# Z and the output stage of a convolution and token-mixing kernel moved from whole-array matmuls to four 64x64 tiles

## The chip, the core and the metric

The kernel runs on one core of one Trainium2 chip. The metric is the device time of that core in microseconds (us), lower is better. It is given as the median of several executions. Fast executions of one kernel agree here within about 1% (the kernel before on one chip: 180.46 to 182.05 us in seven); some fall into a slower state, with a lower granted TensorE clock in the records (the share of its full clock that the profile says it was given; 0.742 in a run of before of 209.52 us, 0.940 to 0.967 in fast runs of 180.46 to 182.05), or simply a longer time.

## The reference, cut to what matters

```python
batch, seq, d_model, kernel_size, n_heads, d_hyper = 8, 4224, 192, 7, 8, 64

def conv(x, weight):                    # causal convolution, 7 taps, one filter per head of 24 columns
    w = softmax(weight, axis=-1)
    x_pad = concat([zeros(B, 6, D), x], axis=1)
    ...
    return einsum('hk,bskhg->bshg', w, x_unf).reshape(B, S, D)

def mlp(x, w_q, w_k, w_out):            # x is the result of conv
    wq, wk = x @ w_q, x @ w_k
    W_tok = 1 / sqrt(64) * einsum('bsd,btd->bst', wq, wk)
    mixed = einsum('bst,btd->bsd', W_tok, x)
    return relu(mixed) @ w_out          # float32
```

There is no softmax over tokens, so the kernel never forms the 4224 x 4224 matrix. With G = x^T x (192 x 192), `mixed` is (x w_q)(w_k^T G) scaled. Per batch the stages are:

- **Y**: the convolution, as a matmul with a banded matrix.
- **G**: the Gram matrix of Y, summed in one bank of PSUM, the memory that this kernel's matmuls write to (`ps` in the profile). (SBUF is the on-chip memory that they read from: `y`, `zt`, `wall` and others.)
- **T**: Y transposed on VectorE (`STREAM_TRANSPOSE` in the profile, 1,348 ns for 128 x 1,152), to be read in blocks of 32 rows.
- **Q**: w_q^T Y^T, on array tiles of 32 x 64.
- **M**: the 64 x 192 product of w_k and G.
- **Z**: relu(M^T Q), 192 rows for each token.
- **O**: Z^T w_out, the output.

Of the kernel before, what the change touches and what calls it, by code (L numbers as in the profile page):

```python
# [14 lines left out]
KEYS = {  # L15
    "Y": (-0.34, 0.15), "T": (-0.03, 1.15), "Q": (0.07, 0.82), "G": (-0.01, 0.83),
    "Z": (1.01, 0.97), "O": (1.22, 0.93),
}
# [95 lines left out]
def bass_lightweight_conv__then__hypermixer_token_mlp_kernel(  # L114
# [24 lines left out]
    NX = 6  # L139
    NO = 8  # L140
# [19 lines left out]
    ZT = sbuf("zt", [128, NZ, 3, 512], BF16)  # L160
    OUT = sbuf("o_sb", [128, NO, 2, 4 * D], F32)
    GS = sbuf("gs", [128, 512], BF16)
    G12T = sbuf("g12t", [128, 128], BF16)
    M_SB = sbuf("m_sb", [128, 2, 2 * D], BF16)
    BAND = sbuf("band", [128, H, 128], BF16)
    IDENT = sbuf("ident", [128, 128], BF16)
    WST = sbuf("wst", [128, 4, D], F32)
    WALL = sbuf("wall", [128, 1088], BF16)
# [13 lines left out]
    WO1, WO2 = WALL[:, 512:704], WALL[:, 704:1088]  # L182
# [7 lines left out]
    og = [P.group(f"o{i}") for i in range(NO)]  # L190

# [40 lines left out]
    for s, (src, wd) in enumerate(((wk_t, DH), (wo_t, D))):  # L232
        wload(2 * s, 0, 128, src, 0, wd, wl[s + 1])
        wload(2 * s + 1, 0, 64, src, 128, wd, wl[s + 1])
        wload(2 * s + 1, 64, 128, src, 128, wd, wl[s + 1])
# [122 lines left out]
    for o, i, g in (  # L358
        (WO1, WST[:, 2, :], wl[2]),
        (WO2[0:64, 0:D], WST[0:64, 3, :], wl[2]),  # L360
        (WO2[64:128, D : 2 * D], WST[64:128, 3, :], wl[2]),
        (dup(WK1), twice(WST[:, 0, 0:DH]), wl[1]),
        (dup(WK2), twice(WST[:, 1, 0:DH]), wl[1]),
        (dup(WK2A)[0:64], twice(WST[0:64, 1, 0:DH]), wl[1]),
        (dup(WK2B)[64:128], twice(WST[64:128, 1, 0:DH]), wl[1]),
    ):
        wos.append(cast("pool", o, i, g, [wos[-1]]))
    wos.append(pool(lambda e: e.memset(M_SB[:, :, :], 0.0), [wos[-1]]))

# [3 lines left out]
        dve(lambda e: e.memset(ZT[:, :, :, 64:128], 0.0)),  # L373
# [10 lines left out]
    class Job:  # L384
        def __init__(self, name, key, banks, pe, pe_us, reads=(), after=(), evacs=(), then=None,
                     groups=()):
            self.name, self.key, self.banks, self.pe, self.pe_us = name, key, banks, pe, pe_us
            self.reads, self.after, self.evacs, self.then = reads, after, evacs, then
            self.groups = groups
# [64 lines left out]
    def job_q(b, g):  # L454
# [20 lines left out]
        for i0, i1 in ((0, 2), (2, 3), (3, 4)):  # L475
# [30 lines left out]
            after=[("ZD", b - 2, i, h) for i in range(5) for h in range(2)]  # L506
            + [("ZS", b - 2, i) for i in range(5)],
            evacs=evacs,
# [35 lines left out]
    def job_mm(b):  # L544
        def pe(e, bk):
# [11 lines left out]
            after=[("ZD", b - 2, i, h) for i in range(5) for h in range(2)]  # L557
            + [("ZS", b - 2, i) for i in range(5)],
            evacs=[(lambda bk: [
                (M_SB[0:64, b % 2, 0:192], PS[0:64, bk, 0:192]),  # L560
                (M_SB[64:128, b % 2, 256:384], PS[64:128, bk, 0:128]),
                (M_SB[64:128, b % 2, 192:256], PS[64:128, bk, 128:192]),
            ], ("M", b), 480, False, "scale")],
        )

    def blocks(b):
        return (0, 1, 2, 3, 4) if b < B - 1 else (3, 4, 0, 1, 2)

    def nth(b, i):
        return 5 * b + blocks(b).index(i)  # L570

    def zspan(i):
        return (512 * i, 512 if i < 4 else HALF - 2048)

    def zreads(b, i):
        s0, w = zspan(i)
        k = (0, 0, 2, 3, 3)[i]
        q = [("Q", b, 1, 0), ("Q", b, 1, 2)] if i > 2 else []
        return [("M", b), ("Q", b, 0, k), ("Q", b, 1, k)] + q

    def zring_after(n):
        bb, k = divmod(n - NZ, 5)
        ii = blocks(bb)[k]
        return [("O", bb, ii, q) for q in range(2 if ii < 4 else 1)]

    def job_zd(b, i, h):
        s0, w = zspan(i)
        n = nth(b, i)

        def pe(e, bk):  # L590
            return e.matmul(PS[:, bk, 0:w], M_SB[:, b % 2, 256 * h : 256 * h + 128],  # L591
                            QT[:, b % 2, s0 : s0 + w], start=True, stop=True)

        return Job(
            ("ZD", b, i, h), b + KEYS["Z"][0] + KEYS["Z"][1] * (3 * (n % 5) + h) / 15, 1, pe,
            0.42e-3 * w, reads=zreads(b, i), after=zring_after(n),
            evacs=[(lambda bk: [(ZT[:, n % NZ, h, 0:w], PS[:, bk, 0:w])],
                    ("ZD", b, i, h), w, False, "relu")],
        )

    def job_zs(b, i):
        s0, w = zspan(i)
        n = nth(b, i)

        def pe(e, bk):
            return e.matmul(PS[:, bk, 0:w], M_SB[:, b % 2, 128:256], QT[:, b % 2, s0 : s0 + w],  # L606
                            start=True, stop=True)

        return Job(
            ("ZS", b, i), b + KEYS["Z"][0] + KEYS["Z"][1] * (3 * (n % 5) + 2) / 15, 1, pe, 0.42e-3 * w,  # L610
            reads=zreads(b, i), after=zring_after(n),
            evacs=[(lambda bk: [(ZT[:, n % NZ, 2, 0:w], PS[:, bk, 0:w])],
                    ("ZS", b, i), w, False, "relu")],
        )

    def job_o(b, i, q):
        n = nth(b, i)
        zr, orr = n % NZ, n % NO
        rem = i == 4

        def pe(e, bk):
            kw = dict(skip_group_check=True)
            for j in range(1 if rem else 2):
                r = 2 * q + j
                cols = slice(0, 128) if rem else slice(r, 512, 4)
                o = PS[:, bk + j, :]
                for h in range(2):
                    e.matmul(o[:, 192 * h : 192 * h + 192], ZT[:, zr, h, cols], WO1,  # L628
                             start=h == 0, stop=False, **kw)
                last = e.matmul(o[:, 0:384], ZT[:, zr, 2, cols], WO2, start=False, stop=True, **kw)  # L630
            return last

        def make(bk):
            if rem:
                return [(OUT[0:64, orr, :, 0:192],
                         PS[0:64, bk, 0:384].rearrange("p (h d) -> p h d", h=2))]
            return [(
                OUT[:, orr, :, 384 * q : 384 * q + 384].rearrange("p h (r d) -> p r h d", r=2),
                PS[:, bk : bk + 2, 0:384].rearrange("p r (h d) -> p r h d", h=2),
            )]  # L640

        def then():
            halves = n == 5 * B - 1
            if not rem and q == 0 and not halves:
                return
            evs = [o for k in range(q if halves else 0, q + 1) for o in made[("OUT", b, i, k)]]
            row = lambda h, t: (b * S + h * HALF + t) * D
            chunk = [[4 * D, 8], [1, 4 * D]]
            for h in range(2):
                if rem:  # L650
                    parts = [(0, 64, row(h, 17 * CW), [[D, 64], [1, D]])]
                elif halves:
                    parts = [(0, 128, row(h, 32 * i + 2 * q),
                              [[CW * D, 16], [4 * D, 8], [1, 2 * D]])]
                elif i < 3:
                    parts = [(0, 128, row(h, 32 * i), [[CW * D, 16]] + chunk)]
                else:
                    parts = [
                        (0, 96, row(h, 96), [[CW * D, 16], [4 * D, 6], [1, 4 * D]]),
                        (96, 126, row(h, 16 * CW), [[4 * D, 30], [1, 4 * D]]),  # L660
                        (126, 128, row(h, 17 * CW + 64), [[4 * D, 2], [1, 4 * D]]),
                    ]
                for p0, p1, at, dims in parts:
                    src = OUT[p0:p1, orr, h, 0 : D if rem else 4 * D]
                    if halves:
                        src = OUT[:, orr, h, 2 * q * D : 2 * q * D + 2 * D]
                    st = P.dma(
                        "sp",
                        lambda e, src=src, at=at, dims=dims: e.dma_start(
                            bass.AP(out_t, at, dims), src  # L670
                        ),
                        og[orr], evs,
                    )
            st.end = max(o.end for o in evs) + 5.0
# [3 lines left out]
            ("O", b, i, q), b + KEYS["O"][0] + KEYS["O"][1] * (2 * (n % 5) + q) / 9, 1 if rem else 2,  # L678
            pe, 0.33 if rem else 0.655,
            reads=["wo", ("ZD", b, i, 0), ("ZD", b, i, 1), ("ZS", b, i)],  # L680
            evacs=[(make, ("OUT", b, i, q), 384 if rem else 768, False, "copy")],
# [5 lines left out]
        "O": [job_o(b, i, q) for b in range(B) for i in blocks(b)  # L687
              for q in range(2 if i < 4 else 1)],
        "Z": [j for b in range(B) for i in blocks(b)
# [207 lines left out]
```

## The kernel before: the parts that the change touches

A sequence is cut into two halves of 2,112 tokens. Q of one half lies on partitions 0 to 63, that of the other on 64 to 127. Z has 192 rows, which is one and a half times the 128 partitions. The kernel before makes it with three matmuls for 512 tokens of both halves: rows 0 to 127 of the first half, rows 0 to 127 of the second, and rows 128 to 191 of both together. M is padded with zeros, so that one half's M meets zeros in the other half's Q.

```python
def job_zd(b, i, h):          # 128 rows of Z for one half; job_zs: the last 64 rows of both
    def pe(e, bk):
        return e.matmul(PS[:, bk, 0:w], M_SB[:, b % 2, 256 * h : 256 * h + 128],
                        QT[:, b % 2, s0 : s0 + w], start=True, stop=True)
    ...
        evacs=[(lambda bk: [(ZT[:, n % NZ, h, 0:w], PS[:, bk, 0:w])], ..., "relu")]

def job_o(b, i, q):
    def pe(e, bk):
        for j in range(1 if rem else 2):
            r = 2 * q + j
            cols = slice(0, 128) if rem else slice(r, 512, 4)       # every 4th token: step of 8 bytes
            o = PS[:, bk + j, :]
            for h in range(2):
                e.matmul(o[:, 192 * h : 192 * h + 192], ZT[:, zr, h, cols], WO1, ...)
            last = e.matmul(o[:, 0:384], ZT[:, zr, 2, cols], WO2, ...)   # WO2: zeros beside the weights
        return last
```

In this output matmul Z is the stationary operand (the "weights" that are loaded into the array, `LDWEIGHTS ps<-wall,zt` in the profile) and w_out is streamed. Each partition of the output buffer collects four successive tokens, so one store row is 4 x 192 x 4 = 3,072 bytes, and a store takes all 128 partitions:

```python
parts = [(0, 128, row(h, 32 * i), [[CW * D, 16], [4 * D, 8], [1, 4 * D]])]
```

The order of all instructions is fixed when the kernel is built: a list planner in the kernel takes, again and again, the job that is ready and has the lowest key. `KEYS` gives each stage its lead or lag in batches:

```python
KEYS = {"Y": (-0.34, 0.15), "T": (-0.03, 1.15), "Q": (0.07, 0.82), "G": (-0.01, 0.83),
        "Z": (1.01, 0.97), "O": (1.22, 0.93)}
...
rank = (0, job.key) if t <= free["pe"] + 0.05 else (1, t)
```

The kernel takes PSUM as eight banks (`ps`, [128, 8, 512] in float32): G holds bank 7, Q takes four in a row, Y and O take pairs, a Z step takes one.

## Time and profile before

| | before |
|---|---|
| median of 3 runs | 182.16 us (182.05 to 182.72) |
| profiled run | 209.52 us, granted clock 0.742: a slow run |
| a later profile of the same kernel | 181.0 us, granted clock 0.966 |

The first profile is a slow run, and the prediction had only that one. I therefore profiled the kernel before again (run `c_before` below). The profile after was taken in a fast run, so "before" in comparisons of profiles means `c_before`.

How to read the lines: PE is TensorE's matmuls, PEld its weight loads, DVE VectorE, ACT ScalarE. Numbers are us unless they are means of one instruction (ns). The page of the slow profile of before, span, busy time by engine and the chain of waits by engine:

```profile
span 207.8 us, 4686 instructions
...
PE 186.9 (90%) x1911; PEld 125.5 (60%) x1934; DVE 144.9 (70%) x217; ACT 140.4 (68%) x286; POOL 46.6 (22%) x74
...
PE 76%; DMA 8%; DVE 4%; POOL 3%; issue 2%; ACT 2%; SPq 1%; POOLq 0%
```

The table of windows of the same profile, one batch in the middle (its columns are named in its first line):

```profile
core 0: us, PE busy (x) PEld busy (x) DVE busy (x) ACT busy (x) POOL busy (x), PEclk, DMA share, GB/s
105.11:127.53 22.42, 22.06 (x244) 15.29 (x255) 17.13 (x24) 16.91 (x37) 0.00 (x0) 0.75 0.74 180
```

At a clock of 0.75 TensorE alone sets the batch: 22.06 of 22.42 us. The same kernel undisturbed, page of `c_before`; in the lines of the queues the columns are packets, MB and the time that the packets took as a share of 16 engines' span:

```profile
span 179.2 us, 4709 instructions
...
PE 155.2 (87%) x1934; PEld 106.2 (59%) x1934; DVE 143.1 (80%) x217; ACT 136.0 (76%) x286; POOL 46.5 (26%) x74
...
q1 hardware_dynamic: 12016, 26.30, 44.4%
q8 instruction: 15, 0.25, 0.5%
...
PE 46%; DVE 19%; DMA 9%; issue 8%; ACT 6%; POOL 3%; SPq 1%; POOLq 0%
```

Its table of windows, one batch and the end after the last evacuation:

```profile
core 0: us, PE busy (x) PEld busy (x) DVE busy (x) ACT busy (x) POOL busy (x), PEclk, DMA share, GB/s
98.70:116.80 18.10, 17.99 (x240) 12.89 (x239) 16.84 (x24) 16.27 (x37) 0.00 (x0) 1.00 1.33 280
169.00:179.00 10.00, 0.00 (x0) 0.00 (x0) 0.00 (x0) 0.00 (x0) 0.00 (x0) 0.57 0.78 251
```

Here a batch takes 18.1 us, with TensorE busy 99%, VectorE 93% and ScalarE 90% of it. All three are nearly full. The last 10 us only store. Three groups of instructions of `c_before` that the change replaces (count, then busy time and mean ns of one): the output's weight loads, and the ReLU on each engine:

```profile
L796 ACT ACTIVATE zt<-ps 128x512 bf16<-128x512 f32 x59 | 35.0, 639 | 0.3 <-PE ps L606 0.3
...
L628 PEld LDWEIGHTS ps<-wall,zt 128*128 128x128 bf16 x272 | 27.3, 114 | 15.1 <-DVE y L793 2.0 <-issue 1.9 <-ACT o_sb L793 1.5
...
L798 DVE TENSOR_SCALAR zt<-ps 128x512 bf16<-128x512 f32 x37 | 24.6, 682 | 4.6 <-PE ps L591 4.2
```

### The profile page before, as it was taken

The numbers are of one execution on the slowest core, as the hardware profiler recorded it, in microseconds if no ns is written. First come the engines' busy times: TensorE is split into PE (matmuls) and PEld (weight loads), VectorE is DVE, ScalarE is ACT, GpSimd is POOL, SyncE is SP. The second block draws the span as 40 slices with busy tenths as digits, with TensorE's granted clock in tenths as the row PEclk, the third lists the DMA queues.
The fourth block names the chain that finished last, engine by engine and source line by source line (L and its number), as shares of the span: only waits on it lengthen the run. The fifth ranks groups of instructions, "written<-read, shape, count | busy, mean of one in ns | idle before, by whom it ended". The sixth has DMA issues, their size and how long they took to land.

```text
span 207.8 us, 4686 instructions
## 1 busy us (share of the span) xinstructions
PE 186.9 (90%) x1911; PEld 125.5 (60%) x1934; DVE 144.9 (70%) x217; ACT 140.4 (68%) x286; POOL 46.6 (22%) x74
## 2 busy tenths in 40 slices
PE   7769679999998999999999999999999999999920
PEld 2227435776684667666776676766867677676610
DVE  4894838958894489657975799468965797567410
ACT  2555458668967598667975797669876797567720
POOL 7509999997331000000000000000000000000000
PEclk9776767777777777777777777777777777777775
DMA  5990999999999999999999653383247345459676
GB/s 59 190 149 12 158 189 192 191 192 265 289 276 240 269 265 265 263 230 312 258 237 247 189 153 114 84 278 100 89 143 212 103 143 171 137 171 281 189 251 228
DMA packets 49030, 40.44 MB, mean 195 GB/s; under 512 B 39280, under 2 KB 41072, under 8 KB 49008
## 3 DMA queue, kind: packets, MB, share of 16 engines
q0 software_dynamic: 36992, 13.83, 56.2%
q1 hardware_dynamic: 12016, 26.30, 39.8%
q8 instruction: 15, 0.25, 0.5%
q14 instruction: 7, 0.06, 0.1%
HBM read 28.00 MB, written 25.95 MB: 260 GB/s over the span
## 4 chain that ended last, share of the span: by engine, by line
PE 76%; DMA 8%; DVE 4%; POOL 3%; issue 2%; ACT 2%; SPq 1%; POOLq 0%
PE ps L401 13%; PE ps L628 13%; PE ps L630 12%; PE ps L464 8%; PE ps L515 8%; PE ps L516 6%; DMA xw<-in_x_dram 6%; PE ps L591 6%; PE ps L517 4%; PE ps L606 4%; DVE qt L793 3%; DMA wst<-in_moe_w_out_dram 2%; SPq L220 1%; POOL wall L326 1%; POOL xw L205 1%
## 5 line engine op out<-in xcount | busy, mean ns | idle before, releaser
L791 DVE STREAM_TRANSPOSE yb<-y 128x1152 bf16<-128x1152 bf16 x48 | 62.3, 1348 | 0.4
L793 ACT COPY o_sb<-ps 128x768 f32<-128x768 f32 (+1 forms) x59 | 45.3, 768 | 18.5 <-PE ps L630 16.7
L628 PE MATMUL ps<-wall,zt 128*128 128x192 bf16 x272 | 52.7, 282 | 1.7 <-ACT o_sb L793 0.9
L630 PE MATMUL ps<-wall,zt 128*128 128x384 bf16 x136 | 52.6, 387 | 0.0
L793 ACT CAST y<-ps 128x864 bf16<-128x864 f32 (+3 forms) x76 | 39.7, 586 | 11.4 <-PE ps L401 10.2
L515 PE MATMUL ps<-y 128*128 128x192 bf16 x144 | 40.1, 284 | 2.7 <-DVE y L793 1.3
L401 PE MATMUL ps<-xw,band 126*128 126x432 bf16 x128 | 37.9, 424 | 3.7 <-DMA xw<-in_x_dram 2.4
L628 PEld LDWEIGHTS ps<-wall,zt 128*128 128x128 bf16 x272 | 30.4, 121 | 16.2 <-issue 4.6
L516 PE MATMUL ps<-y 128*128 128x192 bf16 x144 | 40.0, 285 | 0.0
L796 ACT ACTIVATE zt<-ps 128x512 bf16<-128x512 f32 (+1 forms) x76 | 36.7, 535 | 2.4 <-PE ps L606 1.2
L798 DVE TENSOR_SCALAR zt<-ps 128x512 bf16<-128x512 f32 (+1 forms) x44 | 26.1, 613 | 14.0 <-PE ps L591 9.5
L517 PE MATMUL ps<-y 128*128 128x128 bf16 x144 | 35.8, 248 | 0.0
L205 POOL DMA_DIRECT2D xw<-in_x_dram x32 | 30.2, 1005 | 8.5 <-issue 7.7
L793 ACT CAST qt<-ps 128x64 bf16<-128x64 f32 (+4 forms) x46 | 15.0, 397 | 17.1 <-PE ps L464 17.1
L793 DVE CAST y<-ps 128x864 bf16<-128x864 f32 x20 | 21.0, 1052 | 6.5 <-PE ps L401 5.1
L591 PE MATMUL ps<-qt,m_sb 128*128 128x512 bf16 (+1 forms) x59 | 21.0, 393 | 1.2 <-issue 0.8
L401 PEld LDWEIGHTS ps<-xw,band 126*128 126x128 bf16 x128 | 12.3, 107 | 15.5 <-issue 4.0
L516 PEld LDWEIGHTS ps<-y 128*128 128x128 bf16 x144 | 16.1, 112 | 8.9 <-issue 7.3
L793 DVE COPY o_sb<-ps 128x768 f32<-128x768 f32 (+1 forms) x13 | 11.6, 895 | 13.3 <-PE ps L630 13.3
L515 PEld LDWEIGHTS ps<-y 128*128 128x128 bf16 x144 | 15.9, 110 | 8.3 <-issue 2.8
L464 PE MATMUL ps<-yb,wq 32*64 32x288 bf16 x768 | 18.1, 328 | 0.0
L793 DVE CAST qt<-ps 128x224 bf16<-128x224 f32 (+6 forms) x42 | 7.9, 253 | 12.9 <-PE ps L464 12.9
(64 smaller groups left out, 148.3 us busy)
## 6 DMA issues: line engine op xcount, KB each, us to landing
out_dram<-o_sb SPq DMA_DIRECT2D x46, 384.0 KB, 4.2
xw<-in_x_dram POOLq DMA_DIRECT2D x24, 384.0 KB, 20.1
out_dram<-o_sb SPq DMA_DIRECT2D x16, 288.0 KB
xw<-in_x_dram POOLq DMA_DIRECT2D x8, 432.0 KB, 20.2
out_dram<-o_sb SPq DMA_DIRECT2D x16, 90.0 KB
out_dram<-o_sb SPq DMA_DIRECT2D x16, 48.0 KB, 4.9
out_dram<-o_sb SPq DMA_DIRECT2D x4, 192.0 KB
xw<-in_x_dram POOLq DMA_DIRECT2D x16, 29.2 KB, 23.5
```

Source lines behind the costliest of these rows:

```text
L205: return e.dma_start(XW[0:rows, b % NX, slot : slot + n, :], bass.AP(x_t, base, [[D, rows], [CW * D, n], [1, D]]),)
L401: last = e.matmul(PS[:, k + j, 0:432], BAND[0 : 6 + CW, h, :], rhs, start=True, stop=True)
L464: last = e.matmul(PS[64 * h : 64 * h + 64, bk + i, 0:288], WQ[r, j, :], rhs, start=j == 0, stop=j == 5, skip_group_check=True)
L515: e.matmul(PS[:, 7, 0:192], y[:, 0:128], y[:, 0:192], start=c == 0, **fl)
L516: e.matmul(PS[:, 7, 192:384], y[:, 256:384], y[:, 192:384], start=False, **fl)
L517: return e.matmul(PS[:, 7, 384:512], y[:, 128:256], y[:, 128:256], start=False, **fl)
L591: return e.matmul(PS[:, bk, 0:w], M_SB[:, b % 2, 256 * h : 256 * h + 128], QT[:, b % 2, s0 : s0 + w], start=True, stop=True)
L628: e.matmul(o[:, 192 * h : 192 * h + 192], ZT[:, zr, h, cols], WO1, start=h == 0, stop=False, **kw)
L630: last = e.matmul(o[:, 0:384], ZT[:, zr, 2, cols], WO2, start=False, stop=True, **kw)
L791: last = e.transpose(o, i)
L793: last = e.copy(o, i) if eng == "act" else e.tensor_copy(o, i)
L796: last = e.activation(o, i, AF.Relu)
```

## The change

Both Z and O multiply by zeros: Z contracts over 64 rows but uses 128, O contracts over 192 rows but spends the array on 256. The change cuts the array into four 64x64 tiles that hold no zeros. Z is made in three parts of 64 rows (`j`); in each, the array's two row halves take the two sequence halves (`h`) and its two column halves take two blocks of 512 tokens (`g`), so one step is four matmuls at once. The output is summed over the three parts, again with four tiles at once. Each output partition now collects eight successive tokens, so a store row is 6,144 bytes, and a store takes 64 partitions. M needs no padding, and the ReLU empties two banks (1,024 columns) with one instruction. To pay for larger units in memory, the input ring `NX` shrinks from 6 to 5 batches; the output ring keeps its bytes with half as many units of double size. The order keys were set anew, with a penalty for a change of array mode, which is the way the array is cut into tiles.

```diff
 KEYS = {
-    "Y": (-0.34, 0.15), "T": (-0.03, 1.15), "Q": (0.07, 0.82), "G": (-0.01, 0.83),
-    "Z": (1.01, 0.97), "O": (1.22, 0.93),
+    "Y": (-0.82, 0.03), "T": (0.08, 0.78), "Q": (0.17, 0.82), "G": (-0.04, 0.43),
+    "Z": (0.92, 0.82), "O": (1.35, 0.93), "mode": (0.11, 0.13),
 }
-    NX = 6
-    NO = 8
+    NX = 5
+    NO = 4
-    ZT = sbuf("zt", [128, NZ, 3, 512], BF16)
-    OUT = sbuf("o_sb", [128, NO, 2, 4 * D], F32)
+    ZT = sbuf("zt", [128, NZ, 3, 2, 512], BF16)
+    OUT = sbuf("o_sb", [128, NO, 2, 8 * D], F32)
 ... (head: one load of w_out into 64 rows, fewer casts, no padding of M; all else about weights cut)
+    def job_z(b, u, j):
+        def pe(e, bk):
+            for h in range(2):
+                r = slice(64 * h, 64 * h + 64)
+                for g in range(2):
+                    c = 512 * (2 * u + g)
+                    last = e.matmul(PS[64 * g : 64 * g + 64, bk + h, :],
+                                    M_SB[r, b % 2, 64 * j : 64 * j + 64],
+                                    QT[r, b % 2, c : c + 512], start=True, stop=True, ...)
+            return last
+ ...    evacs=[(lambda bk: [(ZT[:, n % NZ, j, :, :], PS[:, bk : bk + 2, :])],
+                ("Z", b, u, j), 1024, False, "relu")],
 ... (job_zr, job_or: the last 64 tokens of each half, the same way)
+    def job_o(b, u, k):
+        v, q = divmod(k, 2)
+        def pe(e, bk):
+            for rr in range(2):
+                for j in range(3):
+                    for h in range(2):
+                        for g in range(2):
+                            p = slice(64 * g, 64 * g + 64)
+                            last = e.matmul(
+                                PS[64 * h : 64 * h + 64, bk + g, 192 * rr : 192 * rr + 192],
+                                ZT[p, zr, j, h, slice(4 * v + 2 * q + rr, 512, 8)],
+                                WO[p, j, :], start=rr == 0 and j == 0, stop=j == 2, ...)
 ... (then(): stores after the fourth output step, 64 partitions each)
+                        c = [[CW * D, 16], [8 * D, 4 if i < 3 else 3], [1, 8 * D]]
+                        parts.append((OUT[64 * h : 64 * h + m, orr, g, :], row(h, 32 * i), c))
-            rank = (0, job.key) if t <= free["pe"] + 0.05 else (1, t)
+            change = 0.0
+            if job.pe and job.mode != mode[0]:
+                change = KEYS["mode"][0]
+                t += 0.1
+            rank = (0, job.key + change) if t <= free["pe"] + 0.15 else (1, t)
```

## The prediction

> **What bounds the kernel now.** The profiled run is a slow one (span 207.8 us, granted clock 0.742; the timed runs took 182.16). In it TensorE bounds everything between the head and the tail: in the table of windows each batch repeats every 22.42 us with TensorE busy 22.0, VectorE 17.1, ScalarE 16.9; the chain of waits is 76% TensorE. I count 39,744 streamed columns per batch (band filter 6,912, Gram 9,216, Q 3,456, Z 6,336, output 13,056, rest 768). In the timeline an output pair of 768 columns repeats every 0.43 us, 1.79 columns per ns; so 39,744 columns are 22.2 us, and almost nothing is left for mode changes or gaps. The head (first matmuls of batch 1 at 27 us, waiting for x, which was issued after the weights' casts) and the store tail (199.5 to 207.8) hardly follow the clock. So a fast run has (180.4-36)/7.67 = about 18.8 us per batch. There VectorE and ScalarE (34.0 us together, 17.0 each) are 90% busy and TensorE is about as full: three engines bind together.
>
> **What the change removes.** Z needs 6 x 512 columns plus a remainder instead of 6,336, output 17 x 576 instead of 17 x 768: 6,300 columns per batch, 16%: 3.5 us at the slow clock, about 2.6 at the full one. This needs four 64x64 tiles to run together; [...]the Q stage agrees here: 48 matmuls of 288 columns on 32x64 tiles took 1.14 us, so eight overlapped.
>
> Evacuation: the elements stay, instructions fall. Six pairs of 512-wide ReLU (ScalarE 617 ns, VectorE 688) become 1,024 wide (extrapolated from 512 and 768 wide: 0.99 and 1.23 us), saving 0.15 to 0.25 us each; three remainders become one, three M copies one: together about 1.9 us of 34 per batch, 0.95 per engine.
>
> Head: two weight loads, a 0.74 us memset and some casts leave the chain before x of batch 1: -1 us.
>
> **What it adds.** Three array modes[...]. Four changes per batch cost at most 0.34 us now (22.42-22.08), 0.085 each; I expect 10 to 16: about 1 us. Weight loads: 24 small ones per output step instead of 6, reading Z every 16 bytes instead of 8; loads now take 113 ns strided against 98 contiguous, so a coarser stride may cost more. Z takes bank pairs, so while Q holds four banks only one pair is left. Tail: the last stores leave in 0.75 MB pieces rather than 0.38 MB, at 360 GB/s: +1 us.
>
> **On the critical path.** TensorE per batch (fast) about 14 + 1 = 15; evacuation 16 per engine. Evacuation becomes the bound; at 92% use a batch takes 17.3 us instead of 18.8: 7.67 x 1.5 = -11.5; head -1, tail +1. Predicted 170.5 us, range 162 to 179; faster by over 2% 0.80, within 2% 0.12, slower 0.08.
>
> **What would show it.** Right: batch period (slow clock) 19 to 20 us; four output matmuls starting within one 192-column time; VectorE and ScalarE over 85% busy; ReLU of 1,024 near 1.0 and 1.2 us; TensorE idle waiting for evacuation. Wrong: an output step well above 0.64 us at the slow clock (weight loads bound it), gaps over 0.1 us at mode changes, long waits for free banks.
>
> **What would make it wrong.** Weight loads not hidden or serial between tiles (then output gains nothing and it may be slower); mode changes of 0.2 us or more; the after profile in another clock state; a tail longer than 10 us.

Beside it:

- -11.5 - 1 + 1 from 182 gives 170.5.
- That tiles overlap rested on the Q stage: in the first profile the 48 matmuls of a Q step start in groups of eight within 24 ns, and the groups follow one another after 123 to 173 ns.
- The price of 0.085 us for a change of mode and the +1 us for the tail are estimates: 0.34 us of a batch over four changes, and 0.37 MB more at the rate of the tail of before (windows of the first profile: 371 GB/s from 200 to 202 us, 359 from 202 to 204).
- That head and tail hardly follow the clock held for the head: the first band matmuls of batch 1 start at 27.0 us in the slow profile and in `c_before`. From the last matmul to the end it is 9.5 and 11.7 us.

## The result, and the profile after

| | before | after |
|---|---|---|
| median | 182.21 us, 4 runs | 213.85 us, 4 runs |
| ratio of fast runs | | 1.170 (1.161 to 1.178) |
| span of the fast profile | 179.2 (`c_before`) | 212.6 |
| granted clock in it | 0.966 | 0.932 |

The change made the kernel 17% slower. A ratio is the mean time of one kernel's fast runs over that of the other's in the same rounds, so it is not quite the ratio of the medians that I quote. One of the four runs after (218.04 us) is slow and is left out of it. Experiments ran on chips 2, 3 and 5 (the record doesn't name the chip of this pair), each beside runs of the kernel before; differences to after are therefore given by the medians and, in brackets, by the ratios, as a share of 182 us.

The page of after, the lines that answer to those of `c_before`:

```profile
span 212.6 us, 7380 instructions
...
PE 166.0 (78%) x3326; PEld 115.7 (54%) x3326; DVE 132.9 (63%) x192; ACT 140.9 (66%) x231; POOL 46.1 (22%) x72
...
q1 hardware_dynamic: 7840, 26.25, 46.0%
q8 instruction: 26, 0.43, 0.8%
...
PE 63%; DMA 9%; ACT 6%; DVE 5%; POOL 4%; issue 4%; SPq 1%; POOLq 0%
```

No engine is full any more: VectorE is busy 63%, ScalarE 66%. The instruction queue carries 26 packets instead of 15, beside 3,326 matmuls and as many loads on TensorE instead of 1,934. The windows of after, four batches and the end:

```profile
core 0: us, PE busy (x) PEld busy (x) DVE busy (x) ACT busy (x) POOL busy (x), PEclk, DMA share, GB/s
71.40:94.80 23.40, 20.42 (x415) 14.25 (x413) 15.60 (x22) 17.45 (x29) 0.00 (x0) 0.93 1.38 260
94.80:119.90 25.10, 20.70 (x415) 14.54 (x413) 15.47 (x22) 17.32 (x29) 0.00 (x0) 0.93 0.83 182
119.90:140.60 20.70, 19.22 (x415) 13.72 (x413) 15.44 (x22) 17.06 (x29) 0.00 (x0) 1.00 0.66 159
140.60:161.20 20.60, 19.37 (x415) 13.82 (x413) 15.51 (x22) 17.16 (x29) 0.00 (x0) 1.00 0.66 158
195.00:212.00 17.00, 0.00 (x0) 0.00 (x0) 0.00 (x0) 0.00 (x0) 0.00 (x0) 0.57 0.79 197
```

Two kinds of batch stand out: calm ones of 20.6 us at the full clock, and two of 23.4 and 25.1 us, at a clock of 0.93, in which x is still arriving (its last packet starts at 106.3 us, halfway through the second). The tail, in which only stores run, is 17 us instead of 10, at 197 GB/s instead of 251. The groups of instructions of after:

```profile
L632 PE MATMUL ps<-wo,zt 64*64 64x192 bf16 x1536 | 57.7, 287 | 2.3 <-DVE zt L839 0.8 <-DVE qt L834 0.8 <-issue 0.3
...
L632 PEld LDWEIGHTS ps<-wo,zt 64*64 64x64 bf16 x1536 | 51.3, 209 | 10.4 <-issue 1.9 <-ACT o_sb L834 1.3 <-DVE zt L839 1.3
...
L837 ACT ACTIVATE zt<-ps 128x1024 bf16<-128x1024 f32 x43 | 44.0, 1029 | 12.8 <-PE ps L587 12.1
...
L587 PEld LDWEIGHTS ps<-qt,m_sb 64*64 64x64 bf16 x192 | 6.1, 113 | 15.2 <-ACT o_sb L834 6.1 <-issue 3.7 <-ACT zt L837 2.2
...
L839 DVE TENSOR_SCALAR zt<-ps 128x1024 bf16<-128x1024 f32 x5 | 6.1, 1224 | 3.8 <-PE ps L587 3.8
```

Compare the two kinds of 64x64 load: one of Z's weights (contiguous, line 587) takes 113 ns, one of the output's (every eighth token, line 632) takes 209. The timeline of TensorE in after, a calm stretch and a disturbed one (start, duration, then what ran; consecutive equal instructions are joined):

```profile
start us, us, engine line op out<-in xcount [idle before <-releaser]
...
127.14 0.22 PE L524 MATMUL ps<-y 128*128 128x128 bf16 x1
127.30 1.68 PE L632 MATMUL ps<-wo,zt 64*64 64x192 bf16 x48
128.80 0.39 PE L587 MATMUL ps<-qt,m_sb 64*64 64x512 bf16 x4
...
97.33 0.40 PE L587 MATMUL ps<-qt,m_sb 64*64 64x512 bf16 x1
100.91 0.41 PE L587 MATMUL ps<-qt,m_sb 64*64 64x512 bf16 x3 [3.18 <-issue]
```

In the calm stretch 48 output matmuls, 12 groups of four, went in 128.80 - 127.30 = 1.50 us, 125 ns for a group; 192 columns at the full clock would be 80: in this trace band matmuls of 432 columns start 182 ns apart and Gram matmuls of 128 columns 55, so 304 columns more take 127 ns, 2.4 per ns. In the disturbed one TensorE stopped for 3.2 us **inside** a group of four matmuls that wait for nothing.

What the clock of 0.93 is made of: about 1 us after each of the two long gaps (at 74.9 and 97.3 us) the granted clock was halved for 3.4 us, and band matmuls of 432 columns started 351 to 360 ns apart instead of about 182. Windows of after on these two stretches, columns as above:

```profile
78.10:81.40 3.30, 3.30 (x38) 1.82 (x35) 0.96 (x1) 2.47 (x3) 0.00 (x0) 0.50 1.44 264
101.90:105.30 3.40, 3.40 (x39) 2.20 (x35) 0.00 (x0) 2.63 (x5) 0.00 (x0) 0.50 0.74 130
```

In `c_before` there is no such stretch between 30.4 us and the tail. So these two gaps came with a loss beyond their length; that they caused it isn't shown: a gap of 2.1 us in `e5_cols4` (at 72.2 us) has no such stretch after it.

### Where TensorE's time went

I counted TensorE's time in the traces from matmul start to matmul start, from 27 us to the last matmul. "Columns" is the streamed columns over 2.4 per ns, the full rate worked out above. What a change of mode adds, up to 0.1 us, is "modes". "Loads" are other losses under 60 ns, "starts" the few ns by which tiles of one group start after one another, and "waits" everything longer. What runs slower at half the clock falls into loads and waits: 5.4 us of columns (at the full rate) ran so in after (26.8 to 33.7 us and the two stretches above), 1.7 in `c_before`, 1.2 in `e5_cols4`. So about 3.8 us of what after lost against before is the clock. (`e1`, `e5` and `e7` are experiments below.)

| us | columns | modes | loads | starts | waits | sum |
|---|---|---|---|---|---|---|
| before (`c_before`) | 124.6 | 2.9 | 2.7 | 2.1 | 8.3 | 140.5 |
| after | 101.5 | 11.1 | 10.8 | 8.0 | 35.1 | 166.5 |
| `e1_contig` | 101.4 | 11.1 | 0.5 | 8.7 | 34.5 | 156.1 |
| `e5_cols4` | 101.7 | 11.1 | 0.9 | 8.4 | 29.8 | 151.8 |
| `e7_flips` | 124.6 | 13.6 | 4.1 | 2.1 | 7.9 | 152.3 |

The columns fell by 23 us (21.5 over the whole run, as intended; after does 1.4 us more of them before 27 us), and everything else rose by 49. The span grew by 33.4 us: 26 of them are in this stretch, 7.2 after the last matmul (11.7 us to the end before, 18.9 after).

By what stood next, the 35.1 us of waits in after are 8.9 before Y, 8.1 before Z, 8.2 before O, 7.8 in gaps like the one at 97.3 us, and 2 others. Two obvious suspects are not in the profile: after 33 us no matmul of after or of `e5_cols4` waits for x, so the smaller input ring did not hold TensorE up, and no wait of TensorE, VectorE or ScalarE is put down to a store.

### The profile page after: what moved, and what is told of

Read it like the earlier page. It is cut to its first block, busy times and chain, and to the rows that moved or that the text cites. A ratio compares the mean times of both kernels' runs of the same rounds, so it can differ in the third digit from the quotient of the medians.

```text
span 212.6 us, 7380 instructions
## 1 busy us (share of the span) xinstructions
PE 166.0 (78%) x3326; PEld 115.7 (54%) x3326; DVE 132.9 (63%) x192; ACT 140.9 (66%) x231; POOL 46.1 (22%) x72
## 3 DMA queue, kind: packets, MB, share of 16 engines
q1 hardware_dynamic: 7840, 26.25, 46.0%
## 4 chain that ended last, share of the span: by engine, by line
PE 63%; DMA 9%; ACT 6%; DVE 5%; POOL 4%; issue 4%; SPq 1%; POOLq 0%
PE ps L632 24%; PE ps L409 10%; PE ps L522 7%; DMA xw<-in_x_dram 7%; PE ps L472 6%; PE ps L587 6%; PE ps L523 5%; PE ps L524 3%; DVE o_sb L834 3%; ACT o_sb L834 3%; POOL xw L211 2%; DMA wso<-in_moe_w_out_dram 2%; DVE zt L839 2%; PE ps L695 1%; ACT y L834 1%
## 5 line engine op out<-in xcount | busy, mean ns | idle before, releaser
L632 PE MATMUL ps<-wo,zt 64*64 64x192 bf16 x1536 | 57.7, 287 | 2.3 <-DVE zt L839 0.8
L632 PEld LDWEIGHTS ps<-wo,zt 64*64 64x64 bf16 x1536 | 51.3, 209 | 10.4 <-issue 1.9
L837 ACT ACTIVATE zt<-ps 128x1024 bf16<-128x1024 f32 x43 | 44.0, 1029 | 12.8 <-PE ps L587 12.1
L834 ACT COPY o_sb<-ps 128x768 f32<-128x768 f32 x49 | 38.5, 799 | 14.0 <-PE ps L632 13.4
L522 PE MATMUL ps<-y 128*128 128x192 bf16 x144 | 34.8, 254 | 1.7 <-DVE y L834 1.2
L523 PE MATMUL ps<-y 128*128 128x192 bf16 x144 | 34.2, 251 | 0.0
L524 PE MATMUL ps<-y 128*128 128x128 bf16 x144 | 32.1, 223 | 0.0
L211 POOL DMA_DIRECT2D xw<-in_x_dram x32 | 30.4, 1025 | 2.8 <-issue 2.0
L587 PE MATMUL ps<-qt,m_sb 64*64 64x512 bf16 x192 | 19.8, 394 | 10.6 <-ACT o_sb L834 5.0
L834 DVE COPY o_sb<-ps 128x768 f32<-128x768 f32 x15 | 14.4, 958 | 20.2 <-PE ps L632 20.2
L834 DVE CAST y<-ps 128x864 bf16<-128x864 f32 (+3 forms) x22 | 21.3, 975 | 7.5 <-PE ps L409 6.6
L522 PEld LDWEIGHTS ps<-y 128*128 128x128 bf16 x144 | 14.2, 99 | 13.2 <-issue 8.0
L834 ACT CAST qt<-ps 128x64 bf16<-128x64 f32 (+4 forms) x36 | 12.3, 402 | 9.7 <-PE ps L472 9.7
L523 PEld LDWEIGHTS ps<-y 128*128 128x128 bf16 x144 | 14.4, 100 | 1.9 <-issue 0.4
L524 PEld LDWEIGHTS ps<-y 128*128 128x128 bf16 x144 | 14.4, 100 | 0.0
L587 PEld LDWEIGHTS ps<-qt,m_sb 64*64 64x64 bf16 x192 | 6.1, 113 | 15.2 <-ACT o_sb L834 6.1
## 6 DMA issues: line engine op xcount, KB each, us to landing
xw<-in_x_dram POOLq DMA_DIRECT2D x24, 384.0 KB, 17.1
xw<-in_x_dram POOLq DMA_DIRECT2D x8, 432.0 KB, 17.3
```

Of the source, the lines that this page charges most:

```text
L211: return e.dma_start(XW[0:rows, b % NX, slot : slot + n, :], bass.AP(x_t, base, [[D, rows], [CW * D, n], [1, D]]),)
L522: e.matmul(PS[:, 7, 0:192], y[:, 0:128], y[:, 0:192], start=c == 0, **fl)
L523: e.matmul(PS[:, 7, 192:384], y[:, 256:384], y[:, 192:384], start=False, **fl)
L524: return e.matmul(PS[:, 7, 384:512], y[:, 128:256], y[:, 128:256], start=False, **fl)
L587: last = e.matmul(PS[64 * g : 64 * g + 64, bk + h, :], M_SB[r, b % 2, 64 * j : 64 * j + 64], QT[r, b % 2, c : c + 512], start=True, stop=True,
L632: last = e.matmul(PS[64 * h : 64 * h + 64, bk + g, 192 * rr : 192 * rr + 192], ZT[p, zr, j, h, slice(4 * v + 2 * q + rr, 512, 8)], WO[p, j ...
```

## The experiments

The theories, with the letters that the expectations use:

- **A**: the output's weight loads read every eighth bf16 and are too slow to hide (209 ns against 113 for the contiguous ones).
- **B**: stores from 64 partitions move more slowly than stores from 128 (the tail at 197 GB/s instead of 251).
- **C**: changes of array mode cost about 0.1 us each, and there are nearly four times as many (119 against 32).
- **D**: the loads of x, which keep the DMA engines busy (a share of 1.38 in the window from 71.4 us), make the long gaps of TensorE inside a group and the long batches.
- **E**: the order of instructions, planned with durations that the chip doesn't show, makes the waits.
- **F**: Z needs pairs of neighbouring PSUM banks, and only few pairs are free.

A control came first.

### The kernel before once more: `c_before`

Edit: none.

> The kernel before once more, unchanged, for a profile in the fast state (its first profile fell in the slow state, clock 0.742). If TensorE at the full clock and the two evacuating engines bind together, the batch period is about 18.8 us and the clock in calm stretches 1.0. If the fast state were a clock of about 0.88, the period would still be about 18.9 us but TensorE would be over 95% busy. Needed to set the steady period of after (20.6 us in a fast run) against the right number.

Measured: 181.0 us, clock 0.966, the profile shown above. A batch takes 18.2 us, close to the 18.8 that the prediction had worked out for a fast run, and three engines are indeed near full. So the reading of before was sound.

### Theory A: contiguous weight loads, `e1_contig`

```diff
-    ZT[p, zr, j, h, slice(4 * v + 2 * q + rr, 512, 8)],
+    ZT[p, zr, j, h, slice(64 * (4 * v + 2 * q + rr), 64 * (4 * v + 2 * q + rr) + 64)],
```

The tokens land in wrong rows; the result is wrong, the work is the same.

> After, with the weights of the output's matmuls read from 64 neighbouring columns of Z instead of every 8th column (wrong result on purpose; same counts, same waits). Theory A, weight loads with a 16-byte step bound the output: the four-matmul groups repeat every 80 ns instead of 120, the load's own time falls from 213 to about 106 ns, an output step of 24 matmuls falls from 0.72 to 0.48 us, 1.9 us per batch, so up to 15 us of the span (about 199 us); not all of the 31 us. Rival, small weight loads or matmul pairs have a floor whatever the step: the groups stay at 120 ns and the time at 214.

Measured: 206.56 us (205.97 to 209.85), ratio to before 1.137 (1.130 to 1.145), so 7.3 us less than after (5.9 by the ratios). Groups of `e1_contig`, output matmuls and their loads:

```profile
L632 PEld LDWEIGHTS ps<-wo,zt 64*64 64x64 bf16 x1536 | 32.5, 108 | 13.1 <-issue 3.2 <-DVE zt L839 1.6 <-ACT zt L837 1.5
...
L632 PE MATMUL ps<-wo,zt 64*64 64x192 bf16 x1536 | 43.0, 248 | 3.7 <-issue 1.4 <-DVE zt L839 1.1 <-DVE qt L834 0.8
```

The load falls from 209 to 108 ns on average, and groups of four start every 83 ns instead of every 120. In the table above the loss of loads falls from 10.8 to 0.5 us, and the last matmul comes 10 us sooner. A is shown. Not all of it reaches the end: the time from the last output copy to the end grew from 17.6 to 20.7 us: the stores end last in both, and their packets in the tail still took 74 ns per KB.

### Theory A, the size of the step: `e4_strides`

The step of the loads differs from batch to batch in one kernel (wrong result on purpose, one look):

```diff
+    def zcols(b, r):
+        st = (8, 8, 8, 4, 2, 1, 8, 8)[b]
+        a = 64 * st * (r // st) + r % st
+        return slice(a, a + 63 * st + 1, st)
-    ZT[p, zr, j, h, slice(4 * v + 2 * q + rr, 512, 8)],
+    ZT[p, zr, j, h, zcols(b, 4 * v + 2 * q + rr)],
```

> After, with the column step of the output's weights chosen per batch: 8, 8, 8, 4, 2, 1, 8, 8 for batches 0 to 7 (wrong result on purpose in batches 3 to 5). Theory A[...]: the period of a group of four is 120 ns at step 8 and about 80 ns (the 192 columns) at steps 2 and 1, and at step 4 between 80 and 90. Rival (a floor of the load): 120 ns in all batches. One look, no times.

Measured (medians over the batches of each step), 211.51 us in one run:

| step in bf16 elements (bytes) | load, ns | group of four matmuls, ns |
|---|---|---|
| 8 (16) | 213 | 120 |
| 4 (8) | 133 | 83 |
| 2 (4) | 107 | 83 |
| 1 (2) | 107 | 83 |

A step of 4, which the kernel before had too, costs a little in the load and nothing in the groups. The cliff lies between 8 and 16 bytes. At a step of 4 a load took 133 ns and not 107, though the matmuls hid it (83 ns for a group); at a step of 8 it took 213 ns, twice as long, and the groups 120.

### Theory B: stores from all partitions, `e2_full128`

```diff
-  parts.append((OUT[64 * h : 64 * h + m, orr, g, :], row(h, 32 * i), c))
   ... (and the other cases)
+            for vv in vs:
+                for g in range(2):
+                    parts.append((OUT[:, orr, g, 768 * vv : 768 * vv + 768], area(g, vv), whole))
```

Each store takes all 128 partitions with rows of 3,072 bytes, the same bytes to wrong places (wrong result).

> After, with every large store taken from all 128 partitions in rows of 3,072 bytes instead of from 64 partitions in rows of 6,144 (same bytes, same number of large stores; the rows land at wrong places on purpose). Theory B, [...]packets in calm stretches go from 74 to about 40 ns per KB, the tail after the last output copy from 18 to about 10 us, so about 205 us. Rival, the tail is the issue time of the stores or their late release: the packets or the tail stay and the time stays at 214.

Measured: 197.74 us (196.88 to 199.0), ratio 1.092 (1.085 to 1.098), 16.1 us less than after (14.2 by the ratios). Page of `e2_full128`, span and the queue of the stores:

```profile
span 195.8 us, 7344 instructions
...
q1 hardware_dynamic: 11360, 26.25, 36.3%
```

Its window in the tail, columns as in the windows above:

```profile
188.00:195.00 7.00, 0.00 (x0) 0.00 (x0) 0.19 (x1) 0.00 (x0) 0.00 (x0) 0.64 0.79 310
```

The tail runs at 310 GB/s instead of 197, and the time from the last output copy to the end falls from 17.6 to 7.7 us. The engines' time for the same 26.25 MB falls from 46.0% of 16 x 212.6 = 1,565 us to 36.3% of 16 x 195.8 = 1,137. Counted in the trace in a calm stretch, a packet took 444 ns for 6,144 bytes in after (74 ns per KB) and 40.7 ns per KB here. While x is loading at the same time (60 to 100 us), the same packets of after took 247 ns, 41 ns per KB, so there no extra cost of the narrow stores shows.

B is shown, for 10 us of tail. The last copy came 6.8 us sooner too (195.0 to 188.2), although nothing on TensorE had changed: waits fell from 35.1 to 27.5 us, of which gaps like that at 97.3 us from 7.8 to 4.4. Most of the rest is the clock: no stretch at half the clock stands between 29.5 us and the tail, and the columns that ran at half the clock fell from 5.4 to 1.4 us. That the narrow stores made those gaps longer is not shown: this is one profile of each kernel, and gaps of this kind differ between profiles (below).

### Both mended in a correct kernel: `e5_cols4`

The two column tiles of the output step need not be the two sequence halves. If they are two groups of 64 tokens of one half, one partition needs only four successive tokens, as before, the step is 4, and a store takes 128 partitions:

```diff
-    NO = 4
+    NO = 8
-    OUT = sbuf("o_sb", [128, NO, 2, 8 * D], F32)
+    OUT = sbuf("o_sb", [128, NO, 2, 4 * D], F32)
-        v, q = divmod(k, 2)
+        h, q = divmod(k, 2)
-                    for h in range(2):
+                    for v in range(2):
                         for g in range(2):
+                            c0 = 256 * v + 2 * q + rr
-                                PS[64 * h : 64 * h + 64, bk + g, ...],
-                                ZT[p, zr, j, h, slice(4 * v + 2 * q + rr, 512, 8)],
+                                PS[64 * v : 64 * v + 64, bk + g, ...],
+                                ZT[p, zr, j, h, slice(c0, c0 + 253, 4)],
 ... (stores after every second step, as the kernel before makes them)
```

> A correct kernel: after, but the two output halves of a four-tile step are two groups of 64 tokens of one sequence half instead of the two sequence halves. So the weights' step is 4 columns instead of 8, each store covers 128 partitions in rows of 3,072 bytes, and it can leave after two output steps instead of four. Theories A and B together: groups every 83 ns, calm store packets 40 ns per KB, tail about 9 us. From the two single runs (7 and 16 us below after) about 190 us if they add, a little less for the earlier stores. If the two overlapped, 196 or more. Still slower than before, since 119 changes of array mode (32 before, 0.096 us each) are left: 8 us of TensorE time.

Measured: correct, 193.74 us (193.29 to 195.16), ratio 1.072 (1.064 to 1.081). That is 20.1 us less than after (17.8 by the ratios) and still 12.3 more than before beside it. Windows of `e5_cols4`, two calm batches, columns as above:

```profile
111.00:131.20 20.20, 17.65 (x414) 11.83 (x413) 15.38 (x22) 16.86 (x29) 0.00 (x0) 1.00 0.58 170
131.20:150.10 18.90, 17.75 (x415) 11.81 (x413) 15.47 (x22) 16.82 (x29) 0.00 (x0) 1.00 0.62 179
```

Its group of the output's loads:

```profile
L633 PEld LDWEIGHTS ps<-wo,zt 64*64 64x64 bf16 x1536 | 34.7, 135 | 13.4 <-issue 4.0 <-DVE zt L828 1.8 <-ACT zr L826 1.4
```

The load is 135 ns, store packets take 40.3 ns per KB, the tail is 11.7 us. What A and B cost is gone, and the kernel is still slower than before. Against `c_before` its TensorE stretch has 22.9 us less of columns and 1.8 less of loads, but 8.2 more of modes, 6.3 more of starts and 21.5 more of waits.

### Theory C alone: mode changes in the kernel before, `e7_flips`

Eight tiny matmuls of one column on a 64x64 tile, with zero weights, in each batch, between whole-array steps of the kernel before. They add 128 changes of mode and almost no columns; the result stays correct.

```diff
+            if c % 2 == 1 and c < NCK - 1:
+                last = e.matmul(PS[0:64, 7, 0:1], WARM[0:64, 0:64], WARM[0:64, 0:1], start=False,
+                                stop=False, skip_group_check=True)
```

> Before, with eight one-column 64x64 matmuls of zeros per batch put between the Gram steps (they add zero; the result stays correct): 16 more changes of mode per batch, 128 in all, and nothing else. Theory C, each change costs TensorE about 0.096 us and TensorE is nearly full: 128 x 0.096 = 12 us of TensorE time[...]; of 18.2 us per batch only about 1 is free, so the run is 5 to 13 us slower (186 to 194). Rival, the changes hide in waits for evacuation: under 2 us.

Measured: 193.31 us (191.39 to 194.38), ratio 1.064 (1.055 to 1.073): 11.9 us more than before beside it, 0.093 us for a change with its share of the tiny matmul. Window of `e7_flips`, one batch:

```profile
86.10:105.80 19.70, 19.64 (x253) 13.55 (x253) 17.02 (x24) 16.46 (x37) 0.00 (x0) 1.00 1.35 272
```

The batch grew from 18.1 to 19.7 us. What the trace shows lost at changes of mode in a batch grew from 0.38 to 1.95 us, 0.098 per added change, so hardly any of the cost is elsewhere. In after the median lost at a change is 96 ns as well. C is shown. After's modes are 8.2 us more than before's.

### Theory D: no loads of x, `e8_noload` and `e11_cols4_noload`

After and `e5_cols4`, without the loads of x for batches 5 to 7 (which compute on old x; wrong):

```diff
-            groups=[xg[b][0], xg[b][1]] if g == 0 else [xg[b][2]],
+            groups=[xg[b % NX][0], xg[b % NX][1]] if g == 0 else [xg[b % NX][2]],
...
+        if b >= NX:
+            break
         load(b, 0, 0, 1, xg[b][0], old)
```

> After, without the x loads of batches 5 to 7 (they read what batches 0 to 2 left; wrong result on purpose; all compute stays). Theory D, the long TensorE gaps in the middle of a matmul group (1.9 us at 75 and 3.6 us at 97)[...] and the first batches (23.4 and 25.1 us against 20.6 later) pay for the loads: with the loads over at about 70 us, batches from then on take 20.6 us and the gap at 97 is gone: 5 to 8 us less, about 207. Rival, the schedule itself makes those batches longer: the time stays at 214.

> The kernel e5_cols4 without the x loads of batches 5 to 7 (wrong result on purpose). [...]4 to 7 us less, about 188; the gaps at places 1985 to 3521 shrink. If they no longer lie on the path: under 2 us.

(Measured times: in `e8_noload` the two gaps and the two long batches, in `e11_cols4_noload` the gaps at every 256th instruction of TensorE, whose sum I then put at 7.8 us.)

Measured for `e8_noload`: 206.14 us (205.42 to 207.25), ratio 1.139 (1.131 to 1.146), 7.7 us less than after (5.6 by the ratios). Its windows over the two batches that were long in after:

```profile
71.20:91.40 20.20, 18.97 (x415) 13.63 (x413) 15.45 (x22) 17.05 (x29) 0.00 (x0) 1.00 0.68 163
91.40:111.70 20.30, 19.07 (x421) 13.65 (x420) 15.54 (x22) 17.15 (x29) 0.00 (x0) 1.00 0.68 163
```

They are 20.2 and 20.3 us instead of 23.4 and 25.1, and the gaps at 75 and 97 us are gone, with the halved clock after them. But not all such gaps are: one of 1.4 us stands at 112.6 us and one of 2.6 us at 172.9, over 50 and 110 us after the last packet of x (58.3 us), at a share of 0.70 of the DMA engines (172 to 176 us); 3.4 us at half the clock follow the second (176.7 to 180.1). Timeline of `e8_noload`:

```profile
172.86 0.26 PE L608 MATMUL ps<-qt,m_sb 64*64 64x32 bf16 x11
175.59 0.17 PE L608 MATMUL ps<-qt,m_sb 64*64 64x32 bf16 x1 [2.47 <-issue]
```

For `e11_cols4_noload`: 189.54 us (189.0 to 191.02), ratio 1.043 (1.036 to 1.050), 4.2 less than `e5_cols4` (5.3 by the ratios), with gaps of this kind at 3.7 us instead of 8.7. Without x the kernel is still slower than before, which does load x.

What are these gaps? I numbered the instructions of TensorE (loads, matmuls and the semaphore waits between them) in order. In after the gap of 1.9 us at 74.9 us lies at number 1985, that of 3.6 us at 97.3 us at 2753, a smaller one at 3521. In `e5_cols4` there are gaps at 1217, 1729, 1985, 2753, 3009 and 3521. All these numbers leave the remainder 193 when divided by 256, give or take one. So do those of the two gaps of `e8_noload` just named (3521 and 6081). In all eleven profiles of kernels with the four tiles, among them four with other orders, the places with this remainder and the next collect the most time of all 256. The queue that the page calls "instruction" moved 26 packets of 16,384 bytes beside 6,691 of the numbered instructions in after, 15 beside 3,892 in the first profile of before: one for 257 and for 259. And transfers of that queue stand beside the two large gaps, at 74.5 and 98.6 us. Before, with 3,868 loads and matmuls instead of 6,652, shows no such gap, though its DMA engines are as busy (a share of 1.33 in the window shown, 1.38 in the first of after), and neither does `e7_flips`. So the place is shown: the stops of TensorE lie at multiples of 256 instructions from one another. What it waits for there is not shown: the trace names no releaser ("issue"). That x makes the stops is shown in part only: without it their sum fell in `e5_cols4` from 8.7 to 3.7 us, but in `e8_noload` one of the longest came long after x. No run changed the instruction count alone, so why before never stops stays open.

### Theory E: the order, `e9_oldkeys`, `e10_order`, `e13_early`

`e9_oldkeys` is `e5_cols4` with the order keys of the kernel before (one round):

```diff
-    "Y": (-0.82, 0.03), "T": (0.08, 0.78), "Q": (0.17, 0.82), "G": (-0.04, 0.43),
-    "Z": (0.92, 0.82), "O": (1.35, 0.93), "mode": (0.11, 0.13),
+    "Y": (-0.34, 0.15), "T": (-0.03, 1.15), "Q": (0.07, 0.82), "G": (-0.01, 0.83),
+    "Z": (1.01, 0.97), "O": (1.22, 0.93), "mode": (0.11, 0.13),
```

> The kernel e5_cols4 with the order keys of before (mode key kept). It tells how much of the loss at the start (batch 1's bands stand at 30 us instead of 27) and of the waits comes from the order alone: if the new order is at fault, 3 to 6 us faster than e5_cols4; if its grouping by mode pays (136 changes here against 119), 2 to 6 us slower.

`e10_order` is `e5_cols4` with the planner's durations set to those that the traces show (arrival of x, Z and output steps, evacuations), and keys searched anew with them:

```diff
-    "Y": (-0.82, 0.03), "T": (0.08, 0.78), "Q": (0.17, 0.82), "G": (-0.04, 0.43),
-    "Z": (0.92, 0.82), "O": (1.35, 0.93), "mode": (0.11, 0.13),
+    "Y": (-0.988, 0.023), "T": (0.059, 1.227), "Q": (0.208, 0.586), "G": (-0.084, 0.867),
+    "Z": (0.477, 1.293), "O": (1.346, 1.069), "mode": (0.088, 0.13),
...
-    COST = {"act": (0.1, 0.833e-3, 0.833e-3), "dve": (0.1, 1.04e-3, 0.52e-3)}
+    COST = {"act": (0.17, 0.833e-3, 0.833e-3), "dve": (0.16, 1.04e-3, 0.52e-3)}
```

> The correct kernel e5_cols4 with a new order of the same instructions: the planner that lays the order down gets the durations of the traces (evacuations 0.06 to 0.07 us longer each, an output step 0.525 us, x of batch b at the times it really landed) and order keys chosen for them; 125 changes of mode. Theory E, the waits of 2.2 us per calm batch for bank pairs and the late first batches come from an order laid down for other durations: 4 to 9 us less than e5_cols4 (185 to 190). Rival, the waits belong to the bank pairs themselves: within 2 us of e5_cols4 (193.7).

`e13_early` is `e10_order`, with x of batch 1 requested before the casts of the weights, and keys searched again:

```diff
+    load_all(1, z_later)
     wos = [ident]
```

> The kernel e10_order with x of batch 1 asked for before the casts of the weights, its order laid down for that, and only 107 changes of mode. If the first 30 us (TensorE waits for x of batch 1) and the mode changes are what is left, another 3 to 8 us less than e10_order: 178 to 186, about as fast as before. If the order made at the desk does not hold on the chip, no gain over e10_order.

Measured: `e9_oldkeys` 195.36 us (2 runs), ratio 1.079 (1.067 to 1.090), its verdict unclear; the mode changes rose from 119 to 136. `e10_order` 196.17 us (195.62 to 198.2), ratio 1.082 (1.073 to 1.091): no gain over the 1.072 (1.064 to 1.081) of `e5_cols4`. `e13_early` 202.55 us (198.81 to 205.81), ratio 1.095 (1.086 to 1.105) from its two fast runs, two others and the profile being slow: a miss. In `e10_order` the waits sum to 29.4 us as in `e5_cols4` (29.8), only elsewhere: before the output 10.5 instead of 4.2, gaps 256 instructions apart 3.9 instead of 8.7. E, as "a better order of the same jobs would win the time back", has no support: three other orders gave nothing.

### Theory F: bank pairs, `e14_zscatter`

`e5_cols4`, with a Z step in any two free banks, the seventh among them, each emptied by an instruction of its own, as before:

```diff
-  PS[64 * g : 64 * g + 64, bk + h, :],
+  PS[64 * g : 64 * g + 64, bk[h], :],
...
-  evacs=[(lambda bk: [(ZT[:, n % NZ, j, :, :], PS[:, bk : bk + 2, :])],
-          ("Z", b, u, j), 1024, False, "relu")],
+  evacs=[(lambda bk, h=h: [(ZT[:, n % NZ, j, h, :], PS[:, bk[h], :])],
+          ("Z", b, u, j, h), 512, False, "relu") for h in range(2)],
```

> The correct kernel e5_cols4, but Z's four-tile step takes any two free banks, the seventh among them, and each bank is evacuated by an instruction of its own, 512 wide (as before), on whichever engine is free; matmuls and tiles as in e5_cols4. Theory F, TensorE's waits in e5_cols4 for banks (5.5 us before Z and 5.0 us before the bands in the middle batches) come from taking and freeing banks in pairs with one bank unused: those waits fall by half or more and the run is 3 to 7 us less (187 to 191), though evacuation pays about 0.2 us more per step. Rival, the waits come from the order or the evacuation itself: within 2 us of 193.7.

Measured: correct, 194.88 us (194.29 to 196.66), ratio 1.074 (1.068 to 1.081), the same as `e5_cols4`. The waits before Z did fall, from 8.0 to 5.0 us, and those before Y from 8.0 to 6.3; but those before the output rose from 4.2 to 9.1. F falls as stated: more free banks moved the waits and hardly shortened their sum (29.8 to 29.1). (With other banks the planner also lays down another order, with 131 changes of mode instead of 119.)

## Why the prediction was wrong

**What was right.**

- The bound of before: fast batches were estimated at 18.8 us with three engines near full; 18.2 measured.
- The columns: 2.6 us less per batch at the full clock; measured 16.56 to 13.96, which is 2.6.
- The tiles do overlap: the four matmuls of a group start within 10 ns of each other.
- The evacuations: ReLU of 1,024 predicted at 0.99 us on ScalarE and 1.23 on VectorE, measured 1.03 and 1.22; VectorE and ScalarE together predicted at 32.1 us per batch, measured 15.5 + 17.1 = 32.6.
- The number of mode changes: "10 to 16" per batch at about 0.085 us; measured 119 in all, about 15 per batch, at 0.096. The term of 1 us was 1.6.

**The step that failed** is the sum on the critical path: "TensorE per batch (fast) about 14 + 1 = 15; evacuation 16 per engine. Evacuation becomes the bound; at 92% use a batch takes 17.3 us instead of 18.8". The calm batches of the traces, in us, before from 80.5 to 116.8 us, after from 119.9 to 161.2, `e5_cols4` from 111.0 to 150.1, halved:

| us per calm batch | columns | modes | loads | starts | own work | waits | batch |
|---|---|---|---|---|---|---|---|
| predicted | 14 | 1 | 0 | 0 | 15 | | 17.3 |
| before | 16.56 | 0.38 | 0.37 | 0.28 | 17.59 | 0.57 | 18.16 |
| after | 13.96 | 1.64 | 1.45 | 0.93 | 17.97 | 2.69 | 20.65 |
| `e5_cols4` | 13.86 | 1.64 | 0.03 | 1.01 | 16.53 | 2.98 | 19.51 |

1. *Loads and starts were in the sum at zero.* TensorE's own work in after is 17.97 us, not 15, and thus not less than before's 17.59: the modes, the loads and the starts ate all of the columns saved. The prediction had named a coarser stride as a danger ("weight loads not hidden") and seen that loads took 113 ns strided against 98 contiguous, but priced it at nothing. A step of 16 bytes doubled the load (213 against 107 ns, `e4_strides`), and that cost 10 us of TensorE's time (`e1_contig`).
2. *Evacuation did not become the bound.* Its work was sized well (32.6 us for both engines against 32.1), but it was to fill 92% of the batch (16 of 17.3 us), and VectorE and ScalarE are busy 75% and 83% of a calm batch. TensorE, which was to be the emptier engine, stayed the fullest, and its use fell from 97% (17.59 of 18.16) to 87% (17.97 of 20.65). Without the loads' cost, in `e5_cols4`, its own work is 16.53 us and the batch still 19.51: so a second mistake was to take it for granted that some engine would stay near full. Why none did is open (below).
3. *The tail* was priced at +1 us, by size of the last piece. It is +7.2: the packets of 6,144 bytes, from 64 partitions, took 445 ns in it, 74 per KB, and with stores from all 128 (`e2_full128`, 40.7 ns per KB in a calm stretch) 9.9 us of it went away.
4. *The head* was to be 1 us shorter, by fewer casts. x of batch 1 is indeed issued 1.1 us sooner (17.7 instead of 18.8 us), and the first eight band matmuls of batch 1 start at 26.0 instead of 27.0 us. But in the new order all sixteen stand together: TensorE waits 1.6 us for the second half of x and begins the other eight at 30.4 us, at half the clock. (That is the 30 us that an expectation above sets against 27: the link of the critical chain, not the first matmul.)
5. *The gaps 256 instructions apart*, 7.8 us in after, and the halved clock after the two longest (3.4 us each), were not foreseen at all. With 2,784 more loads and matmuls on TensorE the instruction queue carried 11 more packets; what the gaps come from is not shown.

**What stays open.** The correct kernel without A and B is still 12 us slower than before. Of that, modes (+8.2), starts (+6.3) and the gaps 256 instructions apart (8.7) are measured, against 23 of columns saved. The other 13 us or so of added waits, where steps wait for banks and for evacuations, moved from stage to stage under other orders and under free choice of banks, but did not shrink. That they come from fewer and larger steps, each of which holds more until it is emptied, would fit; no run shows it. No correct version that I ran beat the kernel before; the best is `e5_cols4` at 193.74 us.

## What to carry to other kernels

Counting the columns that a tiling saves is only the first line of the sum: price each change of array mode (0.096 us here), each strided weight load at its new byte step (133 ns at 8 bytes, 213 at 16, 107 at 2 and 4), and the gaps that may come with more instructions on TensorE (7.8 us in after, none seen in before), and compare the engine's own work per period with that of before, not with its columns. A layout chosen for the matmul also decides from how many partitions the results leave (in calm stretches 74 ns per KB from 64 here, 40.7 from 128), so look at the store's shape as part of the change. And this kernel with three engines near full did not keep their use when its steps and their order changed; test that first with a cheap variant.
